# Interleaving the second DFT stage of ssm_k with the first DFT stage of kv, in one shared buffer

## The chip, the cores and the metric

The kernel runs on one core of a Trainium2 chip. The core has a matrix engine (TensorE, written PE below; its weight loads are written PEld), a vector engine (VectorE, DVE), an activation engine (ScalarE, ACT), a general engine (GpSimd, POOL) and a queue that starts the transfers (SyncE, SP). Every engine takes its instructions in the order in which the program wrote them, and waits where an operand isn't ready or a buffer isn't free. In this kernel TensorE reads its operands from the memory SBUF and writes its results to PSUM, in tiles of one or two banks (a bank holds 512 fp32 values in each of 128 partitions). DVE and ACT empty PSUM into SBUF; POOL works on data in SBUF alone.

The metric is the device time of one launch in microseconds (us). Before the change it was 207.4 us, the median of three runs from 207.04 to 207.55. A profile is one further execution. Its span was 204.4 us (206.56 us by the clock of the time measurement), so differences between points of the profile are read as differences of the time.

## The reference

Inputs are bf16, with 2048 tokens and 512 channels. The kernel computes a pre-normalised H3 block followed by a dense block:

```
ln(x)  = (x - mean) / sqrt(var + 1e-5)               over the channels
kv     = (sum_t shift(k, t) * shift_k[:, 3-t]) * v   4 causal taps
y      = irfft(rfft(pad(kv)) * rfft(pad(ssm_k)))[:2048]     length 4096, along the tokens
y      = bf16(y) + kv * ssm_D
h      = A_q + ln(A_q) * y
out    = h + relu(ln(h) @ w1) @ w2
```

The long convolution takes two forward transforms, one of the filter `ssm_k` and one of `kv`, a product of the spectra, and one inverse transform.

## The kernel before, in words

The kernel does each transform as two stages of matrix products. A row of 2048 values is seen as 64 rows of 32. Stage 1 (`stage1`) is a short transform over one index, with tables `f1`/`f2` kept as a bf16 high part and a bf16 low part, so that each result is a sum of two products. It gives 64 "planes" c: 32 frequencies k1, each with a real and an imaginary plane. Stage 2 (`stage2`) is a transform over the other index. For each k1 it multiplies the two planes of that k1, 128 partitions by 256 columns each, with 128x128 tables `cc`, `cs`, `cn` in the replicated fp32 format (fp32r), and gives the real part (s = 0) or the imaginary part (s = 1).

The order of the work is written by hand. The part around the change runs as follows.

1. Eight rounds of `taps` (the 4-tap convolution of k, times v) and `stage1(kfl, a1k, gb, ...)`, the first stage of ssm_k. Round gb writes columns 32*gb to 32*gb+31 of all 64 planes of `a1k`.
2. `to_rows` turns kv into the layout `xfl` with TensorE transposes.
3. The k4 loop: eight rounds of the second stage of ssm_k. Each round makes four k1, in two PSUM tiles `ps2k` of two banks. The tile of s = 0 is emptied by DVE, which adds `dcol` (the ssm_D term), and the tile of s = 1 by ACT; both go to `kf`, the spectrum of the filter.
4. Eight rounds `stage1(xfl, a1x, gb, ...)`, the first stage of kv. Each round fills two PSUM tiles `ps1` of two banks; ACT empties the first into `a1x` and DVE the second, through the helper `copy` (its lines appear in the profile as L258 for ACT and L260 for DVE). In round 4 the second tile is split between DVE and ACT.
5. The product stage: 16 rounds of `product(kp)` (second stage of kv into `u`, then the products with `kf` on DVE and POOL) and `finish` (sums into `psy`, emptied by ACT back into `kf`). Then the inverse transform and the dense block follow.

`a1k` and `a1x` are both tiles of 64 KB per partition from the pool `slotA`, which has one buffer. So the first write to `a1x` must wait until the last product of step 3 has read `a1k`: steps 3 and 4 can't overlap.

In steps 3 and 4 the four PSUM places `ring` = 1, 3, 2, 0, of two banks each, are given out in turn. A place can be written again when its eviction is done.

`stage1` has two forms. With `pairs=True` it works on 64 rows at a time: 8 groups x 2 tables x 2 halves = 32 products with 128 columns each. With `pairs=False` it works on 32 rows at a time: 8 x 2 x 4 = 64 products with 64 columns each. The four 32-row products, or the two 64-row ones, lie in different rows of TensorE's array. Step 4 uses pairs in rounds 1 to 7, and the 32-row form in round 0.

In the old plane order the real planes are c = k1 and the imaginary ones c = 32 + k1. `stage2` therefore reads planes k1 and 32 + k1, which lie 32 KB apart in each partition.

Of the kernel before, what the change touches and what calls it, by code (L numbers as in the profile page):

```python
# [12 lines left out]
F32R = mybir.dt.float32r  # L13
I32 = mybir.dt.int32
PSUM = bass.MemoryType.PSUM
P = 128
# [40 lines left out]
def kernel(  # L57
# [13 lines left out]
    nc = tc.nc  # L71
    _, S, D = A_q.shape
# [4 lines left out]
    DC = D // P  # L77
# [8 lines left out]
    slotA = pl.push("slotA")  # L86
# [52 lines left out]
    def _sin(out, turns, M, neg=False):  # L139

        nc.scalar.activation(out=out, in_=turns, func=ACT.Sin, scale=(-TURN if neg else TURN) / M,
                             bias=(pbias if neg else nbias)[:])
# [35 lines left out]
    def at_k1(tab, k1):  # L178
        a, t = [p for p in tab if p[0] <= k1][-1]
        return t[:, k1 - a, :]  # L180
# [25 lines left out]
    t1 = early.tile([P, 64], I32, name="f1_t")  # L206
    _turns(nc, t1[:, 0:32], r1[:], n1c[:], 128, True)
    _turns(nc, t1[:, 32:64], r1[:], n1c[:], 128, False)
    f1f = early.tile([P, 64], F32, name="f1_f")
    _sin(f1f[:, 0:32], t1[:, 0:32], 128)  # L210
    _sin(f1f[:, 32:64], t1[:, 32:64], 128, neg=True)
    t3 = early.tile([P, 2, 64], I32, name="dm_t")
    _turns(nc, t3[:, 0, :], r2[:, 32:96], n2s[:], 64, True)
    _turns(nc, t3[:, 1, :], r2[:, 32:96], n2s[:], 64, False)
# [9 lines left out]
    def cc_part():  # L224
        table(*cc_parts.pop(0))
# [21 lines left out]
    def negated(a, b):  # L247
        (ao, to), (ai, ti) = [[p for p in tab if p[0] <= a][-1] for tab in (cn, cs)]
        nc.gpsimd.tensor_single_scalar(out=to[:, a - ao:b - ao, :], in_=ti[:, a - ai:b - ai, :].bitcast(F32), scalar=-1.0,
                                       op=ALU.mult)  # L250
# [5 lines left out]
    def copy(eng, o, i):  # L256
        if eng == "A":
            nc.scalar.copy(out=o, in_=i)  # L258
        else:
            nc.vector.tensor_copy(out=o, in_=i)  # L260
# [9 lines left out]
    def bank2(name):  # L270
        return place([P, 2, 512], F32, name)
# [19 lines left out]
    def stage1(fl, a_out, gb, engs, pairs=False):  # L291

        pss = [bank2("ps1") for _ in range(2)]
        n, tabs = 2 if pairs else 4, (f2hi, f2lo) if pairs or fl is not kfl else (f1hi, f1lo)
        K = P // n
        for gi in range(8):
            for f in range(2):
                for t in range(n):
                    rows = slice(K * t, K * t + K)
                    cols = slice(0, P)  # L300
                    if pairs:
                        o = pss[t][:, gi // 4, 128 * (gi % 4):128 * (gi % 4) + 128]
                    else:
                        if fl is not kfl:
                            cols = slice(64 * (t % 2), 64 * (t % 2) + 64)
                        else:
                            cols = slice(0, 64)
                        o = pss[t // 2][:, t % 2, 64 * gi:64 * gi + 64]
                    nc.tensor.matmul(out=o, lhsT=fl[rows, 8 * gb + gi, :, :].rearrange("p d n -> p (d n)"),  # L309
                                     rhs=tabs[f][rows, cols], start=(f == 0), stop=(f == 1),  # L310
                                     tile_position=(K * t, 0), skip_group_check=True)
        for h in range(2):
            if pairs:
                src = pss[h][:].rearrange("p b (g r c) -> p c (b g) r", g=4, r=2)
            else:
                src = pss[h][:].rearrange("p r (g c) -> p c g r", c=64)
            dst = a_out[:, :, 32 * gb:32 * gb + 32].rearrange("p c (g r) -> p c g r", r=DC)[:, :, :, 2 * h:2 * h + 2]
            for g, eng in enumerate(engs[h]):
                n = 8 // len(engs[h])
                copy(eng, dst[:, :, g * n:g * n + n], src[:, :, g * n:g * n + n])  # L320

    def stage2(ps, a_in, kp, s):

        for kk in range(2):
            k1 = 2 * kp + kk
            w_re, w_im = ((cc, cs), (cn, cc))[s]
            nc.tensor.matmul(out=ps[:, kk, :], lhsT=at_k1(w_re, k1), rhs=a_in[:, k1, :], start=True, stop=False,  # L327
                             skip_group_check=True)
            nc.tensor.matmul(out=ps[:, kk, :], lhsT=at_k1(w_im, k1), rhs=a_in[:, 32 + k1, :], start=False, stop=True,  # L329
                             skip_group_check=True)  # L330


    kfl = early.tile([P, 64, 2, 64], BF16, name="kfl")
# [11 lines left out]
    dim = consts.tile([P, 2, 2, 64], F32R, name="dim")  # L345
    nc.gpsimd.memset(dre[:].bitcast(F32), 0.0)
    nc.gpsimd.memset(dim[:].bitcast(F32), 0.0)
    a1k = slotA.tile([P, 64, 256], F32R, tag="A", name="a1k")


    kvp2 = sk[:].rearrange("p c t -> p (c t)").rearrange("p (m c a e) -> p m c a e", m=32, c=DC, e=2)
    def taps(c, h):
        pss = [tap_bank(i, [P, 512], F32, "pkv") for i in range(2)]
        for i in range(2):
            for j in range(KS):
                nc.tensor.matmul(out=pss[i][:], lhsT=wdiag[:, 2 * h + i, j, :],  # L356
                                 rhs=kT[c][:, 2 * h + i, 16 - j:CH + 16 - j], start=(j == 0), stop=(j == KS - 1))
        for i in range(2):
            nc.vector.tensor_tensor(out=kvp2[:, :, 2 * h + i, 8 * c:8 * c + 8, :].rearrange("p m a e -> p a m e"),  # L359
                                    in0=pss[i][:].rearrange("p (a m e) -> p a m e", a=8, e=2),  # L360
                                    in1=vT[c][:, 2 * h + i, :].rearrange("p (a m e) -> p a m e", a=8, e=2),
                                    op=ALU.mult)

    for gb in range(8):
        taps(gb // 2, gb % 2)
        stage1(kfl, a1k, gb, ("AA", "AD")[gb % 2], pairs=(gb == 2))
        if gb < 6:
            cc_part()
        if gb == 1:
            negated(22, 32)  # L370
# [18 lines left out]
    xfl = xfp.tile([P, 64, 2, 64], BF16, name="xfl")  # L389
# [7 lines left out]
    for k4 in range(8):  # L397
        ks = slice(4 * k4, 4 * k4 + 4)
        for s in range(2):
            ps = bank2("ps2k")  # L400
            for h in range(2):
                stage2(ps[:, h, :].rearrange("p (k j) -> p k j", k=2), a1k, 2 * k4 + h, s)
            pj = ps[:].rearrange("p b (k j) -> p j (b k)", k=2)
            if s == 0:
                nc.vector.tensor_tensor(out=kf[:, 0, :, ks], in0=pj, in1=dcol, op=ALU.add)
            else:
                nc.scalar.copy(out=kf[:, 1, :, ks], in_=pj)

    a1x = slotA.tile([P, 64, 256], F32R, tag="A", name="a1x")
    for gb in range(8):  # L410
        stage1(xfl, a1x, gb, ("A", "DA" if gb == 4 else "D"), pairs=(gb > 0))
    pl.pop("psX")
    pl.pop("psF")
    pl.pop("xfp")
# [14 lines left out]
    def product(kp):  # L429
        ks = slice(2 * kp, 2 * kp + 2)  # L430
        kfr = kf[:].bitcast(F32)
        ts = []
        for s in range(2):
            u = psu.tile([P, 2, 256], F32, tag=f"u{s}", name=f"u{s}")
            stage2(u, a1x, kp, s)
            usb = prod.tile([P, 256 - NJ, 2], F32, tag=f"usb{s}", name=f"usb{s}", bufs=2)
            uj = u[:].rearrange("p k j -> p j k")
            nc.scalar.copy(out=usb[:], in_=uj[:, po, :])  # L438
            t = prod.tile([P, 2, 256, 2], F32R, tag=f"t{s}", name=f"t{s}")
            for eng, in0, j in ((nc.vector, uj[:, dv, :], dv), (nc.gpsimd, usb[:], po)):  # L440
                n = j.stop - j.start
                eng.tensor_tensor(out=t[:, :, j, :], in0=in0.unsqueeze(1).to_broadcast([P, 2, n, 2]),  # L442
                                  in1=kfr[:, :, j, ks], op=ALU.mult)
            ts.append(t)
        pending.append((kp, ts))
# [19 lines left out]
    for kp in range(16):  # L465
        product(kp)
        if kp >= LAG:
            finish(kp)
        if kp == 7:
            load_x(0)  # L470
            load_x(1)
        if kp == 10:
            w1 = wp.tile([P, DC, DFF], BF16, tag="c2s0", name="w1")
            nc.sync.dma_start(out=w1[:], in_=B_w1.rearrange("(c p) f -> p c f", p=P))
# [357 lines left out]
```

## Time and profile before

The profile's windows (busy time by engine in a stretch) give the stages from the second stage of ssm_k on:

| stretch of the profile, us | what runs | length | PE busy | DVE busy | ACT busy | POOL busy |
|---|---|---|---|---|---|---|
| 38.00 to 52.70 | step 3, second stage of ssm_k | 14.70 | 14.70 | 10.15 | 8.09 | 0.00 |
| 52.70 to 63.70 | step 4, first stage of kv | 11.00 | 8.77 | 9.50 | 10.04 | 0.80 |
| 63.70 to 94.50 | step 5, product stage | 30.80 | 30.72 | 27.38 | 25.25 | 28.24 |
| 94.50 to 114.00 | first inverse stage | 19.50 | 19.19 | 16.01 | 15.77 | 15.47 |
| 114.00 to 204.00 | second inverse stage, dense block | 90.00 | 85.92 | 51.13 | 41.09 | 13.83 |

A busy time is the union of an engine's instructions. Matmuls are pipelined: the start of one to the start of the next is what one costs in a stream, and its listed duration is longer than that. DVE and ACT instructions overlap their neighbours by a little too.

How to read a line of the timeline: start, length, engine, line of the kernel, operation, output<-inputs, shape, count, and in brackets how long the engine had been idle and what released it. A line of the chain: start, length, engine, output and line.

### The profile page before, as it was taken

Reading aid. Unit: us, or ns where it says so; the run is one execution under the profiler, and the core shown is the slowest. Engines: PE = TensorE matmul, PEld = TensorE weight load, DVE = VectorE, ACT = ScalarE, POOL = GpSimd, SP = SyncE. Lnnn points to the kernel's source line nnn. Section 1 sums busy time; section 2 is a strip of 40 time slices with the busy share of each in tenths; the row PEclk is TensorE's granted clock in tenths of the full one; section 3 lists DMA queues with packets and bytes.
Section 4 is the critical chain, followed back from the end, with each engine's and each line's share of the span. In section 5 each row is a group of like instructions: output and inputs, shape, how many; then the busy total and the mean of one; then the engine's idle time right before and its main releaser. Section 6 shows DMA issues by size and latency. Waiting matters only on the chain.

```text
span 204.4 us, 4868 instructions
## 1 busy us (share of the span) xinstructions
PE 194.5 (95%) x1985; PEld 138.0 (68%) x1985; DVE 146.0 (71%) x238; ACT 128.7 (63%) x198; POOL 86.6 (42%) x121
## 2 busy tenths in 40 slices
PE   7989999999997999999999999999999999999991
PEld 2565546999886898897998877545564556544451
DVE  7998777876787999888995698969387117661131
ACT  2768899655896798885979965844570593026300
POOL 7599993000004999996759475110211001002000
PEclk9999999999999999999999999999999999999999
DMA  5999970000000007808990658763483402140011
GB/s 175 343 225 192 192 138 5 3 0 3 5 3 2 0 3 189 264 27 208 203 277 4 109 103 155 138 131 103 92 108 89 116 0 51 32 108 17 0 51 51
DMA packets 48489, 20.01 MB, mean 98 GB/s; under 512 B 43380, under 2 KB 46932, under 8 KB 48468
## 3 DMA queue, kind: packets, MB, share of 16 engines
q1 hardware_dynamic: 47940, 19.71, 44.0%
q8 instruction: 15, 0.25, 0.5%
q10 hardware_dynamic: 528, 0.00, 0.1%
q14 instruction: 6, 0.05, 0.1%
HBM read 7.08 MB, written 2.10 MB: 45 GB/s over the span
## 4 chain that ended last, share of the span: by engine, by line
PE 83%; DVE 5%; ACT 5%; POOL 4%; issue 1%; POOLq 0%; ACTq 0%
PE ps1m L704 19%; PE ps2m L734 19%; PE psy L452 7%; PE psi L599 7%; PE pkv L356 6%; PE ps L309 4%; PE ps2k L327 4%; PE ps2k L329 4%; PE u L327 3%; PE u L329 3%; PE pz L677 3%; PE pst L280 2%; ACT c2s L193 1%; ACT a1x L258 1%; POOL wdiag L237 1%; DVE a1x L260 1%
## 5 line engine op out<-in xcount | busy, mean ns | idle before, releaser
L719 ACT ACTIVATE h1T<-ps1m 128x512 bf16<-128x512 f32 (+1 forms) x44 | 25.7, 597 | 35.8 <-PE ps1m L704 35.7
L704 PE MATMUL ps1m<-xT,w 128*128 128x512 bf16 (+2 forms) x192 | 43.7, 365 | 0.4 <-DVE xT L650 0.4
L734 PE MATMUL ps2m<-w,h1T 128*128 128x512 bf16 (+3 forms) x187 | 40.8, 368 | 0.0
L677 PE MATMUL pz<-bd,ax 128*128 128x128 f32 x96 | 35.7, 410 | 0.0
L442 POOL TENSOR_TENSOR t<-usb,kf 128x320 fp32r<-128x320 f32 x32 | 28.2, 944 | 2.1 <-ACT usb L438 1.7
L442 DVE TENSOR_TENSOR t<-u,kf 128x704 fp32r<-128x704 f32 x32 | 26.7, 886 | 3.1 <-ACT usb L438 3.0
L738 DVE SCALAR_TENSOR_TENSOR o<-ps2m,rstd,xh 128x512 bf16<-128x512 f32 (+1 forms) x17 | 12.1, 717 | 22.9 <-PE ps2m L734 11.5
L734 PEld LDWEIGHTS <-h1T 128*128 128x128 bf16 (+1 forms) x187 | 16.2, 98 | 16.0
L543 POOL TENSOR_SCALAR rstd<-mv 128x4 f32<-128x4 f32 x8 | 2.5, 316 | 56.5 <-DVE mv L541 56.5
L704 PEld LDWEIGHTS <-w 128*128 128x128 bf16 (+1 forms) x192 | 15.9, 100 | 12.1 <-DVE xT L650 0.5
L677 PEld LDWEIGHTS pz<-bd,ax 128*128 128x128 f32 x96 | 18.6, 193 | 7.6
L537 DVE BATCH_NORM_STATS2 st<-xh 128x6 f32<-128x512 bf16 x32 | 19.8, 676 | 0.0
L648 DVE TENSOR_TENSOR qT<-pz,qT 128x1024 bf16<-128x1024 f32 x8 | 9.8, 1220 | 13.6 <-PE pz L677 10.8
L258 ACT CAST kf<-psy 128x512 fp32r<-128x512 f32 x30 | 17.6, 647 | 1.9 <-PE psy L452 0.3
L527 ACT ACTIVATE bd<-ecw,nbias 32x512 fp32r<-32x512 int32 x24 | 17.3, 719 | 0.6
L452 PE MATMUL psy<-t,ipos 128*128 128x512 f32 x48 | 16.0, 393 | 0.0
L356 PE MATMUL pkv<-kT,wdiag 128*128 128x512 bf16 x64 | 15.2, 380 | 0.4 <-POOL f_lo L246 0.4
L258 ACT CAST ax<-psi 128x1024 fp32r<-128x1024 f32 x13 | 12.4, 1015 | 3.7 <-PE psi L599 3.7
L599 PE MATMUL psi<-dre,kf 128*128 128x256 f32 x60 | 14.6, 286 | 0.0
L599 PE MATMUL psi<-dim,kf 128*128 128x256 f32 x60 | 14.3, 280 | 0.0
L258 ACT CAST a1k<-ps 128x1024 fp32r<-128x1024 f32 x12 | 12.5, 1077 | 2.6 <-PE ps L309 2.6
L359 DVE TENSOR_TENSOR sk<-pkv,vT 128x512 bf16<-128x512 f32 x16 | 10.8, 689 | 4.4 <-PE pkv L356 4.2
(134 smaller groups left out, 415.4 us busy)
## 6 DMA issues: line engine op xcount, KB each, us to landing
sk<-in_A_ssm_k_dram SPq DMA_DIRECT2D x1, 2048.0 KB
xh<-in_A_q_dram SPq DMA_DIRECT2D x16, 128.0 KB
out_dram<-o SPq DMA_DIRECT2D x15, 128.0 KB
w<-in_B_w_dram SPq DMA_DIRECT2D x1, 1376.0 KB
w<-in_B_w_dram SPq DMA_DIRECT2D x1, 1280.0 KB
xh<-xT SPq DMA_TRANSPOSE x8
out_dram<-o SPq DMA_DIRECT2D x2, 64.0 KB
w<-in_B_w_dram SPq DMA_DIRECT2D x1, 96.0 KB
```

What stands on the lines that cost most here:

```text
L258: nc.scalar.copy(out=o, in_=i)
L327: nc.tensor.matmul(out=ps[:, kk, :], lhsT=at_k1(w_re, k1), rhs=a_in[:, k1, :], start=True, stop=False, skip_group_check=True)
L356: nc.tensor.matmul(out=pss[i][:], lhsT=wdiag[:, 2 * h + i, j, :], rhs=kT[c][:, 2 * h + i, 16 - j:CH + 16 - j], start=(j == 0), stop=(j == ...
L442: eng.tensor_tensor(out=t[:, :, j, :], in0=in0.unsqueeze(1).to_broadcast([P, 2, n, 2]), in1=kfr[:, :, j, ks], op=ALU.mult)
L452: nc.tensor.matmul(out=psy[:], lhsT=m_[:], rhs=t_.rearrange("p j k -> p (j k)"), start=first, stop=not first)
L527: nc.scalar.activation(out=bd[h][rows, :, :, rg, :], in_=ecw[q % 2][rows, :, 256 * h:256 * h + 256].rearrange("p b (j n) -> p b j n", n=32 ...
L537: nc.vector.bn_stats(out=st[:, i, :], in_=src[:, i, :])
L599: nc.tensor.matmul(out=banks[i // 2][:, i % 2, :], lhsT=kf[:, c, 4 * m:4 * m + 4, :].rearrange("p r k -> p (r k)"), rhs=d[:].rearrange("p ...
L677: nc.tensor.matmul(out=pz[:, il, :, a, :], lhsT=ax[:, 64 * rho + n2, :, :].rearrange("p d g -> p (d g)"), rhs=bd[h][:, rho, 4 * il + a, :, ...
L704: nc.tensor.matmul(out=ps1[fc][:fsz, 128 * ii.start:128 * ii.stop].rearrange("p (i t) -> p i t", t=P), lhsT=w1[:, c, fc * P:fc * P + fsz], ...
L719: nc.scalar.activation(out=h1T[:fsz, fc, :], in_=ps1[fc][:fsz, :], func=ACT.Relu)
L734: nc.tensor.matmul(out=ps2[:, 0:w], lhsT=h1T[:ksz, fc, i * P:(i + 1) * P], rhs=w2[:ksz, fc, ds], start=(fc == 0), stop=(fc == NFC - 1))
```

## The change

The change puts the first stage of kv into the k4 loop. After the two tiles of the second stage of ssm_k for four k1, the loop makes one eighth of the first stage of kv (`gb = k4`). To make that possible in one buffer,

- the planes are reordered so that the real and the imaginary plane of one k1 are neighbours, c = 2*k1 and 2*k1 + 1 (the columns of the table `f1` are written in that order);
- `a1k` and `a1x` become two views of one tile `a1`. As `a1k` it is planes of 256 columns one after the other, so round k4 of the second stage reads planes 8*k4 to 8*k4+7, which are elements 2048*k4 to 2048*k4+2047. As `a1x` it is eight blocks of 2048 elements, one for each gb, with 64 planes of 32 columns in each. So block gb = k4 is free as soon as round k4 has read it;
- the product stage reads a plane of `a1x` as 8 runs of 32 elements, 2048 elements apart, where it was one run of 256;
- all eight groups of kv use the 32-row form, and the split of the second tile between DVE and ACT is made in rounds 2 and 5, not in round 4 alone.

```diff
     f1f = early.tile([P, 64], F32, name="f1_f")
-    _sin(f1f[:, 0:32], t1[:, 0:32], 128)
-    _sin(f1f[:, 32:64], t1[:, 32:64], 128, neg=True)
+    f1p = f1f[:].rearrange("p (k s) -> p s k", s=2)
+    _sin(f1p[:, 0], t1[:, 0:32], 128)
+    _sin(f1p[:, 1], t1[:, 32:64], 128, neg=True)
...
-            dst = a_out[:, :, 32 * gb:32 * gb + 32].rearrange("p c (g r) -> p c g r", r=DC)[:, :, :, 2 * h:2 * h + 2]
+            dst = a_out(gb).rearrange("p c (g r) -> p c g r", r=DC)[:, :, :, 2 * h:2 * h + 2]
...
-            nc.tensor.matmul(out=ps[:, kk, :], lhsT=at_k1(w_re, k1), rhs=a_in[:, k1, :], start=True, stop=False,
+            nc.tensor.matmul(out=ps[:, kk, :], lhsT=at_k1(w_re, k1), rhs=a_in(2 * k1), start=True, stop=False,
                              skip_group_check=True)
-            nc.tensor.matmul(out=ps[:, kk, :], lhsT=at_k1(w_im, k1), rhs=a_in[:, 32 + k1, :], start=False, stop=True,
+            nc.tensor.matmul(out=ps[:, kk, :], lhsT=at_k1(w_im, k1), rhs=a_in(2 * k1 + 1), start=False, stop=True,
...
-    a1k = slotA.tile([P, 64, 256], F32R, tag="A", name="a1k")
+    a1 = slotA.tile([P, 64 * 256], F32R, tag="A", name="a1")
+
+    def a1k_of(gb):
+        return a1[:].rearrange("p (c j) -> p c j", j=256)[:, :, 32 * gb:32 * gb + 32]
+
+    def a1k(c):
+        return a1[:, 256 * c:256 * c + 256]
+
+    def a1x_of(gb):
+        return a1[:, 2048 * gb:2048 * gb + 2048].rearrange("p (c j) -> p c j", j=32)
+
+    def a1x(c):
+        return a1[:].rearrange("p (b c j) -> p b c j", b=8, j=32)[:, :, c, :]
...
-        stage1(kfl, a1k, gb, ("AA", "AD")[gb % 2], pairs=(gb == 2))
+        stage1(kfl, a1k_of, gb, ("AA", "AD")[gb % 2], pairs=(gb == 2))
...
             else:
                 nc.scalar.copy(out=kf[:, 1, :, ks], in_=pj)
-
-    a1x = slotA.tile([P, 64, 256], F32R, tag="A", name="a1x")
-    for gb in range(8):
-        stage1(xfl, a1x, gb, ("A", "DA" if gb == 4 else "D"), pairs=(gb > 0))
+        stage1(xfl, a1x_of, k4, ("A", "DA" if k4 in (2, 5) else "D"))
...
-            stage2(u, a1x, kp, s)
+            stage2(u[:].rearrange("p k (b j) -> p k b j", b=8), a1x, kp, s)
```

## The prediction

> **What bounds the kernel now.** I read the busy time by stretch first, then the chain that ended last where the two stages meet, then the groups by shape in that stretch, then single lines of the timeline for the costs.
>
> By stretch (length, then busy time of PE, PEld, DVE, ACT, POOL):
>
> ```profile
> 38.00:52.70 14.70, 14.70 (x131) 14.62 (x129) 10.15 (x10) 8.09 (x10) 0.00 (x0) 1.00 0.00 1
> 52.70:63.70 11.00, 8.77 (x290) 7.33 (x289) 9.50 (x9) 10.04 (x10) 0.80 (x2) 1.00 0.02 4
> 63.70:94.50 30.80, 30.72 (x193) 27.15 (x194) 27.38 (x33) 25.25 (x62) 28.24 (x32) 1.00 0.33 96
> ```
>
> In the second stage of ssm_k (first line) PE never stops, and DVE and ACT are idle for 4.6 and 6.6 us. In the first stage of kv (second line) it is the other way round: DVE and ACT are nearly full, and PE waits. The product stage (third line) is full on PE again. The chain across the meeting point shows the turn:
>
> ```profile
> 52.75 0.13 PE ps2k L329
> 52.88 0.02 issue
> 52.90 1.02 ACT kf L407
> 53.92 0.04 issue
> 53.96 1.06 PE ps L309 x31
> 55.03 1.09 ACT a1x L258
> 56.12 0.04 issue
> 56.16 2.36 PE ps L309 x64
> 58.52 1.56 ACT a1x L258 x2
> 60.08 0.04 issue
> 60.13 1.06 PE ps L309 x31
> 61.19 0.02 issue
> 61.21 2.37 DVE a1x L260 x2
> 63.58 0.14 issue
> 63.72 0.36 PE u L327
> ```
>
> After 52.88 the end is set by turns of eviction and refill of PSUM. An eviction's end frees a place for PE 0.04 us later, and `u` starts 0.14 us after the last eviction. So 25.65 us (38.07 to 63.72) go to two stages whose busy times complement each other: summed over both, PE 23.5, DVE 19.7, ACT 18.1.
>
> **What the Trainium skill says.** (1) "TensorEngine Tiling (Array Packing)", Key Properties: going from one tiling of the array to another, not only to another tile, drains TensorE. The change has 15 such turns in the loop. The trace agrees, and shows a small price:
>
> ```profile
> 52.59 0.28 PE L329 MATMUL ps2k<-a1k,c2c 128*128 128x256 f32 x1
> 52.80 0.21 PE L309 MATMUL ps<-f_hi,xfl 32*128 32x64 bf16 x4
> 53.41 0.23 PE L309 MATMUL ps<-f_hi,xfl 64*128 64x128 bf16 x1
> ```
>
> A 256-column product takes 0.113 us, so it is done issuing at 52.70; the 32-row group begins at 52.80, a turn of 0.10. The whole 32-row group, with the turn out of it, takes 0.61 (52.80 to 53.41). The pairs groups take 1.06 between turns.
> (2) "SBUF — State Buffer", Specifications: lines of 16 bytes, at least two hits per line for full rate. The runs of 32 fp32 are 128 bytes, eight whole lines, so by this page they cost nothing. The trace has a harder case that agrees: the transposes of ssm_k read single fp32 values 128 bytes apart and start every 0.120 us (ten in 1.35 with a last one of 0.27), those of kv read contiguous ones every 0.113 (eight in 1.06).
> (3) "PSUM — Partial Sum Buffer", PSUM bank collisions: two engines may not read one bank of a partition together. So where a tile is split "DA", the ACT half waits for the DVE half. The trace agrees: the DVE half of round 4 ran 58.56 to 59.24, and the ACT half ended at 60.08, which is what PE waited for.
>
> **The change part by part.** The new table order, the two views and the strides of the first-stage writes change no instruction count and no element count, and in the innermost loops of the writes pairs of adjacent values stay 16 bytes apart: zero. Seven groups of kv go from 32 products of pairs to 64 of 32 rows, so PE gets 448 more instruction entries; at 0.61 for a group of 128 of them, as ssm_k's rounds and kv's round 0 run, that is already counted.
>
> PE, one round of the loop: 16 second-stage products x 0.113 = 1.81; a turn 0.10; the group 0.61; and the first fp32 weight load, which can't be hidden after a turn. The first products of the stage started at 38.07 and 38.29, so that costs 0.22 - 0.11 = 0.11. Sum 2.63 per round.
>
> DVE, one round: `kf` 1.22 and the second kv tile 1.22, which start 1.13 apart if both are waiting (two in 2.35). ACT: `kf` 1.01 and the first kv tile 1.11. Both sums (2.35 and 2.1) lie under PE's 2.63, so they can hide, but the four PSUM places are now used once per round each, and the circuits must be checked. An eviction starts 0.20 after PE has moved on to the next group:
>
> ```profile
> 48.17 0.28 PE L327 MATMUL ps2k<-a1k,c2n 128*128 128x256 f32 x1
> 48.37 1.22 DVE L405 TENSOR_TENSOR kf<-ps2k,dtab 128x1024 fp32r<-128x1024 f32 x1 [0.59 <-PE ps2k L329]
> 53.64 1.23 DVE L260 CAST a1x<-ps 128x1024 fp32r<-128x1024 f32 x1 [0.42 <-PE ps L309]
> ```
>
> and 0.23 after the kv group (53.41 to 53.64).
> - Place of `kf` s = 0: filled at 1.02, evicted from 1.22, but not before DVE is through with the kv tile of the round before: 0.23 + 1.13 = 1.36. End 2.58, free at 2.63. PE wants it at 2.63. It just fits.
> - Place of s = 1: ACT from 2.12 to 3.13; wanted at 2.63 + 1.02 = 3.65. Fits.
> - First kv tile: ACT is busy until 3.1, then to 4.2; wanted at 2.63 + 2.0 = 4.6. Fits.
> - Second kv tile: DVE from 2.86 to 4.08. Fits. In rounds 2 and 5 its ACT half queues behind the first tile, 4.15 to 4.73, so PE waits some 0.1 at the next kv group. Behind that wait only kv's own group stands; `kf`'s next products come after it. Twice, with their effect on the rest: 0.2.
>
> So PE sets the pace. From 38.07: sixteen tiles of eight products 16 x 0.905, eight kv groups with their turn 8 x 0.71, eight weight loads 8 x 0.11; 14.5 + 5.7 + 0.9 = 21.0, and 0.2 gives the end of the last kv group at 59.3. The tail: ACT is still on `kf` until 0.5 after that, then 1.1 for the first kv tile: 60.9, plus 0.14 to `u` = 61.1 instead of 63.7. That is 2.6 us less. Unlike in the old order the tail's evictions are two, not a backlog.
>
> The first kv group can't begin earlier than its input: `xfl` is complete at 39.0, the group starts at 40.1. No wait.
>
> Product stage: the 128 products now read 8 runs. It is full on PE (30.72 of 30.80), so any price is paid in full. From below zero; from above, seven jumps at the 0.007/128 us per jump of the strided transposes are under 0.001 us each product, 0.05 in all. The dense block's moving operand in four runs of 128 shows no price either (first dense stage 9.50/44 = 0.216 a product). I take zero. A jump of 8 KB within a stream of fp32r products isn't in the trace, so I keep up to 0.01 us a product (1.3 us) for the range. Everything after that stage hangs on its end and moves with it, transfers included, since these are released by the product stage's own reads. 207.4 - 2.6 = **204.8**.
>
> **The rivals.**
> - *Turns cost more in this mix* (no fp32 round around a 32-row group exists in the trace twice in a row): at 0.25 a turn in and 0.2 for the weight load the round is 2.87, 1.9 us more over eight, against which the tail shortens a little (ACT is done with `kf` sooner): about 206.4. For it: only one turn of this kind is in the trace. Against: the eight turns between taps and groups in bf16 cost under 0.1 each (period 2.45 for 8 x 0.216 + 0.61).
> - *The PSUM circuit becomes the bound*: the DVE place has no slack. If evictions start 0.35 after the group and not 0.20, the s = 0 circuit gives about 2.73 a round, 0.8 more: 205.6. For it: the first eviction of the stage started 0.35 after. Against: the other seven were at 0.20.
> - *The broken-up reading costs* (ends slower): at 0.03 us a product, 128 x 0.03 = 3.8, time 207.4 + 3.8 - 2.6 = 208.6. For it: PE is full there, and the same fp32r product takes 0.116 there against 0.113 in ssm_k's second stage, so its speed isn't the same in all surroundings. Against: the strided transposes.
> - *Turns hide better than seen*: weight load pulled ahead, 8 x 0.1 less: 204.2.
>
> **How the numbers follow.** Forecast (204.2 to 205.4) 0.6; turns dearer 0.12; PSUM circuit 0.1; broken-up reading 0.1, most of it slower than before; better than 204.2 0.08. The range from 203.7 to 206.5 holds the forecast, the cheap end and both milder rivals, and leaves out the strong form of the reading's price. Faster by over 0.3% means under 206.8: 0.87; same 0.05; slower 0.08.
>
> **What would show it.** In the profile after, `ps2k` and `ps<-xfl` alternate from about 38 us, with rounds of 2.6 to 2.7; the first `u` starts near 61.1; PE's waits in the loop are few and short, the longest before the kv groups of rounds 3 and 6; DVE and ACT are both over 80% busy in the loop. The product stage keeps its length (`u` to the end of `psy` 30.8) and `u` products stay 0.116 apart, and all later stages keep theirs. The forecast is wrong if a round takes 2.9 or more (turns: PE idle with nothing to wait for; circuit: idle released by DVE `kf`), or if the product stage lengthens by over 0.5 us.

## The result, and the profile after

The kernel after takes 204.56 us (204.17 to 205.06, four runs) against 207.48 us for the kernel before (207.04 to 207.75, four runs on the same chip): ratio 0.9863, 95% interval 0.9833 to 0.9892, so 2.9 us less. The forecast was 204.8. The profiled span went from 204.4 to 202.2 us. Some executions fall into a slower state: a median below is that of all runs of a kernel, while each ratio, with its interval, is taken from the fast runs alone.

The windows of the kernel after (stretch, length, then busy time of PE, PEld, DVE, ACT, POOL with instruction counts, PE's clock, DMA share, GB/s) for the loop, the product stage and the rest:

```profile
38.61:61.41 22.80, 21.32 (x643) 19.92 (x641) 18.86 (x18) 17.98 (x20) 0.80 (x2) 1.00 0.02 4
61.41:92.30 30.89, 30.85 (x193) 27.36 (x194) 27.37 (x33) 25.06 (x62) 28.25 (x32) 1.00 0.32 94
92.30:202.20 109.90, 105.16 (x748) 68.43 (x745) 67.26 (x127) 56.93 (x84) 29.35 (x32) 0.99 0.50 96
```

The first of these stretches in the kernel before:

```profile
38.07:63.72 25.65, 23.40 (x419) 21.95 (x417) 19.57 (x18) 18.06 (x19) 0.80 (x2) 1.00 0.01 3
```

From the first `ps2k` to the first `u` there were 25.65 us before; now there are 22.80, which is 2.85 less. That is the whole gain. The other two stretches keep their lengths (30.80 and 109.9 before). In the one profile the loop started 0.54 later than in the profile before, which is why the span shrank by 2.2 and not by 2.9. That start varies between 38.1 and 39.7 over the profiles of this study; in the latest of them, and in this one too, the chain ahead of the loop leads back to the input transfers.

The meeting of one round with the next, in PE's timeline:

```profile
43.13 0.28 PE L330 MATMUL ps2k<-a,c2c 128*128 128x256 f32 x1
43.33 0.21 PE L310 MATMUL ps<-f_hi,xfl 32*128 32x64 bf16 x4
43.37 0.20 PE L310 MATMUL ps<-f_lo,xfl 32*128 32x64 bf16 x4
...
43.95 0.38 PE L328 MATMUL ps2k<-a,c2c 128*128 128x256 f32 x1
44.17 0.28 PE L330 MATMUL ps2k<-a,c2s 128*128 128x256 f32 x1
44.28 0.28 PE L328 MATMUL ps2k<-a,c2c 128*128 128x256 f32 x1
```

The last product of the second stage is through at 43.24 (one takes 0.11), so the turn into the 32-row group costs 0.09. The group with the turn out of it takes 0.62 (43.33 to 43.95), and the first weight load that can't be hidden 0.22 - 0.11 = 0.11. No line has a bracket, so PE waited for nothing. Rounds start at 38.61, 41.30, 43.95, 46.57, 49.23, 51.92, 54.56 and 57.22, so they take 2.62 to 2.69; the second-stage products in them are 0.113 to 0.118 apart.

PE waits once from the loop's start to the product stage, at its end. The view of its waits, and the chain there (start, length, engine, output, line):

```profile
PE u L328 <- ACT a L259: 1.5, 1, 1.5
```

```profile
59.20 0.13 PE ps2k L330
59.33 0.02 issue
59.35 1.01 ACT kf L420
60.36 0.99 ACT a L259
61.35 0.05 issue
61.41 0.38 PE u L328
```

Of the turns of eviction and refill that made up the old chain from 52.88 to 63.72, one is left.

### The profile page after: what moved, and what is told of

Same layout as the page of the kernel before. It is cut to its first block, busy times and chain, and to the rows that moved or that the text cites. A ratio compares the mean times of both kernels' runs of the same rounds, so it can differ in the third digit from the quotient of the medians.

```text
span 202.2 us, 5318 instructions
## 1 busy us (share of the span) xinstructions
PE 192.2 (95%) x2209; PEld 136.3 (67%) x2209; DVE 144.8 (72%) x238; ACT 128.6 (64%) x199; POOL 85.5 (42%) x121
## 4 chain that ended last, share of the span: by engine, by line
PE 78%; SPq 11%; DMA 3%; DVE 3%; ACT 2%; issue 1%; ACTq 0%
PE ps1m L714 19%; PE ps2m L744 19%; PE psy L462 7%; PE psi L609 7%; PE ps2k L328 4%; SPq L118 4%; SPq L115 4%; PE ps2k L330 4%; PE u L328 4%; PE u L330 3%; SPq L117 3%; DMA kT<-in_A_k_dram 3%; PE pz L687 3%; PE ps L310 2%; PE pst L281 2%; PE pkv L369 2%
## 5 line engine op out<-in xcount | busy, mean ns | idle before, releaser
L748 DVE SCALAR_TENSOR_TENSOR o<-ps2m,rstd,xh 128x512 bf16<-128x512 f32 (+1 forms) x17 | 12.1, 717 | 22.2 <-PE ps2m L744 11.5
L259 ACT CAST a<-ps 128x1024 fp32r<-128x1024 f32 (+1 forms) x22 | 22.4, 1054 | 3.6 <-PE ps L310 3.6
L261 DVE CAST a<-ps 128x1024 fp32r<-128x1024 f32 (+1 forms) x12 | 13.6, 1137 | 2.6 <-PE ps L310 2.5
```

## The experiments

### The two halves apart

The change does two things to kv's first stage: it interleaves it, and it puts it into 32-row products. Each was run alone. Interleaving alone:

```diff
-        stage1(xfl, a1x_of, k4, ("A", "DA" if k4 in (2, 5) else "D"))
+        stage1(xfl, a1x_of, k4, ("A", "DA" if k4 in (2, 5) else "D"), pairs=(k4 > 0))
```

> The new order, but kv's groups 1 to 7 as 32 products of 64 rows, as before the change. Theory of the prediction (TensorE sets the round): a round costs 16 x 0.113 + two turns and a weight load 0.21 + 1.06 = 3.08 us, so 7 x 0.45 = 3.2 us come back, and the first u starts near 63.9 us after a start of the loop at 38.07: 207.5 us, level with the kernel before. Rival A (the interleaving alone gives the gain, the smaller products are incidental): at most 205.5 us.

Measured: 207.02 against 207.34, ratio 0.9995 (0.9976 to 1.0015). Interleaving alone gains nothing. Its rounds start 3.01 to 3.02 apart (PE's timeline):

```profile
41.04 0.38 PE L328 MATMUL ps2k<-a,c2c 128*128 128x256 f32 x1
...
44.05 0.38 PE L328 MATMUL ps2k<-a,c2c 128*128 128x256 f32 x1
...
47.07 0.38 PE L328 MATMUL ps2k<-a,c2c 128*128 128x256 f32 x1
```

With pairs PE has 23.82 us of work in a stretch of 25.26 (38.38 to 63.64), so the loop is nearly as long as the two stages were one after the other (25.65). The 64-row groups are too dear on an engine that is now the bound.

32-row products alone, in the kernel before:

```diff
-        stage1(xfl, a1x, gb, ("A", "DA" if gb == 4 else "D"), pairs=(gb > 0))
+        stage1(xfl, a1x, gb, ("A", "DA" if gb == 4 else "D"))
```

> The kernel before, with all of kv's groups as 64 products of 32 rows and nothing else changed. Theory: in the old order that stage waits for evictions, ACT's eight tiles at 1.06 plus a half of 0.55 from 53.9 on, so u starts at about 63.1 instead of 63.7: 206.8 us, 0.6 less. Rival B (the smaller products alone give the gain): 7 x 0.45 less, 204.3 us.

Measured: 212.26 against 207.34, ratio 1.0258 (1.0195 to 1.0321). The expectation was wrong by 5.5 us, and by its sign. To see whether the old layout had a part in it, the same order was run on the layout of after:

```diff
-        stage1(xfl, a1x_of, k4, ("A", "DA" if k4 in (2, 5) else "D"))
+    for gb in range(8):
+        stage1(xfl, a1x_of, gb, ("A", "DA" if gb == 4 else "D"))
```

> The kernel after, with kv's eight groups taken out of the loop again into a loop of their own: new plane order, new layout, broken-up reading and 32-row products, but the old order of stages. Theory (layout and reading cost nothing): like the kernel before with 32-row products, 206.8 us, and u products 0.116 us apart. Rival C (the broken-up reading costs something that the gain hides): slower than that run by 128 times the price, 1.3 us at 0.01.

Measured: 213.49, ratio 1.0267 (1.0181 to 1.0353): the same loss on both layouts, and the same miss, since this expectation was made with the same cost of a group. So the two halves need each other: neither 207.4, interleaved only 207.0, 32 rows only 212.3, both 204.6.

What takes the time is seen in PE's timeline of the kernel with 32-row products alone. These lines stand in the middle of a group, where no operand and no buffer is outstanding:

```profile
57.94 0.21 PE L309 MATMUL ps<-f_lo,xfl 32*128 32x64 bf16 x4 [0.93 <-issue]
...
61.66 0.21 PE L309 MATMUL ps<-f_lo,xfl 32*128 32x64 bf16 x4 [1.53 <-issue]
...
65.39 0.24 PE L309 MATMUL ps<-f_lo,xfl 32*128 32x64 bf16 x4 [1.30 <-issue]
```

PE resumes 3.72 and 3.73 us apart. PE's windows between (busy time and number of products, clock, DMA share, GB/s):

```profile
57.93:61.65 3.72, 1.57 (x128) 1.00 0.02 4
61.65:65.38 3.73, 1.88 (x128) 0.59 0.02 4
```

It ran 128 products in each. A product is two instruction entries, a weight load and a multiplication, so that is 256 entries. The Trainium skill, "Runtime: NRT & Kernel Launch", section "Instruction fetch mechanics", says that an engine's instructions are fetched in blocks of 16 KiB, which are 256 instructions, while it executes the block before, and that this is mostly hidden. The block of 256 agrees with the trace; that it is hidden doesn't hold here. The theory formed on this was: TensorE is fed at most one block per 3.7 us, 69 entries per us. A group of 128 entries is executed in 0.61 us, and groups that follow each other at the pace of the evictions (about 1.2 us) want some 107 per us. The old pairs wanted half of that. In the loop of after a round has 160 entries (16 slow and 64 fast products) in 2.65 us, 60 per us.

The blocks themselves are in the trace. Windows of PE in the kernel with 32-row products alone show them in the last column (GB/s), as little else is transferred here:

```profile
55.50:56.70 1.20, 0.86 (x84) 1.00 0.06 14
56.70:59.05 2.35, 1.27 (x127) 1.00 0.00 0
59.05:60.35 1.30, 0.61 (x36) 1.00 0.06 13
```

13 to 14 GB/s over these lengths are some 17 KB, one block. In the records of the instruction queue (q8), transfers of 16384 bytes start at 55.55, 59.07 and 62.80. PE resumes 2.39, 2.59 and 2.59 us after each of them, and the next one starts 1.13 and 1.14 after PE has resumed. So 3.7 us is one turn of asking for a block and taking it up, and while PE waits no second block is on its way. In the kernel after, five such transfers start in the loop, 3.5 to 5.0 us apart, and PE doesn't wait for them.

A second loss follows from the first. Windows of the same kernel around the end of the stage (the clock is the third number from the end):

```profile
57.00:61.70 4.70, 1.61 (x133) 1.31 (x136) 2.47 (x3) 2.95 (x4) 0.00 (x0) 1.00 0.02 3
61.70:63.50 1.80, 1.25 (x102) 1.08 (x106) 1.35 (x2) 1.39 (x2) 0.00 (x0) 0.67 0.04 9
63.50:67.40 3.90, 1.15 (x64) 0.86 (x62) 2.23 (x2) 1.87 (x2) 0.80 (x2) 0.50 0.01 2
67.40:71.00 3.60, 3.60 (x17) 3.60 (x18) 2.00 (x3) 0.88 (x3) 1.95 (x3) 0.50 0.02 5
```

PE was busy for 1.61 of 4.70 us, and then its clock fell to half. The Trainium skill, "TensorE: Matmul & The Clock Gate", section "What's actually happening", gives half the clock after an idle window of about 3.4 us, and the whole again after as long a busy one. The trace agrees on the half (0.50), and shows that it can fall where PE wasn't wholly idle, and that the whole came back 5.0 us after the full work began. The clock was still down when the product stage began: `u` products were 0.21 apart and not 0.117 until about 72 us. In sum, the stage from the last `ps2k` to `u` took 14.13 us (53.27 to 67.40) where it took 10.97 before, 3.2 more, and the slow products some 2 more: that is about the 4.9 by which the median is longer. The profiled run was the longest of its four, 7.6 over the profiled run before; besides these two losses its loop started 0.5 later, and PE waited 2.0 in the inverse stage for DVE, which it doesn't before.

### The supply of instructions, tested

If the supply is the limit, then the loop of after must starve too once its groups are made twice over, though nothing else in it changes:

```diff
-            for f in range(2):
+            for f in (0, 1) if fl is kfl else (0, 1, 0, 1):
```

> The kernel after with every kv group's products made twice over (the second set starts anew and leaves the same sums): 128 more instruction entries and 0.61 us more of TensorE per round, the same evictions. Theory, TensorE is fed about 256 entries per 3.7 us: a round of 16 slow products and 256 fast ones is 288 entries and takes 4.2 us instead of 3.26, with waits on 'issue' inside the groups; over 8 rounds, less what is in store at the start, 8 to 11 us over the kernel after: 212 to 215. Rival, the waits of the kernels with the groups back to back came from something else (the evictions, the space's buffers): a round costs 2.65 + 0.61 = 3.26 us, with no wait on 'issue': 209.4.

Measured: 217.04 against 207.67, ratio 1.0440 (1.0394 to 1.0486). That is 12.5 over the kernel after (12.0 by the two ratios), where PE's added work alone is 4.9. The waits are back, inside the groups (PE's timeline), and PE again runs a block between one and the next (PE's windows, busy time and count):

```profile
48.73 0.21 PE L310 MATMUL ps<-f_lo,xfl 32*128 32x64 bf16 x4 [0.39 <-issue]
...
52.46 0.21 PE L310 MATMUL ps<-f_lo,xfl 32*128 32x64 bf16 x4 [0.54 <-issue]
...
56.29 0.19 PE L310 MATMUL ps<-f_hi,xfl 32*128 32x64 bf16 x1 [0.64 <-issue]
...
60.02 0.18 PE L310 MATMUL ps<-f_hi,xfl 32*128 32x64 bf16 x1 [0.52 <-issue]
```

```profile
48.72:52.45 3.73, 3.19 (x128) 1.00 0.02 4
52.45:56.28 3.83, 3.19 (x127) 1.00 0.02 4
56.28:60.01 3.73, 3.21 (x128) 1.00 0.02 4
```

The mix of slow and fast products differs from the run before, and so do the buffers and the evictions; the block of 128 products in 3.73 us is the same (one record of the second window is missing). The stalls move through the round, since 288 entries a round is no multiple of 256. The list of queues on the page of the profile counts the blocks, packets first:

```profile
q8 instruction: 17, 0.28, 0.6%
```

```profile
q8 instruction: 21, 0.34, 0.7%
```

The first is after, the second this kernel: four blocks more are 1024 entries, eight rounds of 128. The transfers of the instruction queue start at 46.30, 49.87, 53.59, 57.45 and 61.65, and PE resumes 2.4 to 2.7 us after each. The loop takes 34.27 us (39.07 to 73.34), 11.5 more than after, where the theory allowed 8 to 11. In it stands one wait on "issue" of 2.3 us, longer than the 0.4 to 0.6 of the others: the block ahead of it held fast products almost alone and was done in 1.7 us, and its successor was asked for 1.63 us after PE had resumed, not 1.13 to 1.16. After that wait the clock fell here too, to 0.50 from 65 to 68 us. What each of the two adds isn't separated.

The other side: in the old order, 32 rows in every other group only.

```diff
-        stage1(xfl, a1x, gb, ("A", "DA" if gb == 4 else "D"), pairs=(gb > 0))
+        stage1(xfl, a1x, gb, ("A", "DA" if gb == 4 else "D"), pairs=(gb % 2 == 1))
```

> The kernel before (old order) with 32-row products in kv's groups 0, 2, 4 and 6 and 64-row products in 1, 3, 5 and 7. Theory of supply: 768 entries at 69 per us are 11.1 us, of which the store at the start gives some 150 entries (2 us), so that the evictions of about 10 us set the stage's end: hardly a wait on 'issue', TensorE's clock stays whole, and the time is 206.8 to 207.6. Rival, a 32-row group outside the loop costs some 0.7 us more than a 64-row group whatever stands around it (the loss of 4.9 us over seven groups): three more of them than before, 209.5.

Measured: 208.85 against 207.67, ratio 1.0046 (1.0025 to 1.0066), between the two expectations. The time alone decides nothing; the stage itself does (windows from the last `ps2k` to the first `u`, this kernel and then the kernel before):

```profile
54.40:65.46 11.06, 7.75 (x385) 6.64 (x385) 9.43 (x9) 9.81 (x10) 0.80 (x2) 1.00 0.02 4
```

```profile
52.75:63.72 10.97, 8.72 (x290) 7.36 (x289) 9.45 (x9) 10.04 (x10) 0.80 (x2) 1.00 0.02 4
```

Its length is that of before. PE has no wait on "issue" in it and keeps its clock, with 768 entries in 11.06 us, 69 per us, just at the limit. So a 32-row group outside the loop isn't slow by itself. The stage began 1.65 later in this profile, because the loads at the start came later; the runs of this kernel spread from 206.9 to 209.4 and further. Whether the edit has a part in that isn't settled.

### The price of a turn

The forecast allowed 0.10 for a turn in and 0.11 for the exposed weight load, from one place in the trace before. Here one 32-row product is put ahead of every `ps2k` tile of the kernel with two loops, into a place that is then overwritten:

```diff
             ps = bank2("ps2k")
+            nc.tensor.matmul(out=ps[:, 0, 0:64], lhsT=ident[0:32, :], rhs=f2hi[0:32, 0:64], start=True, stop=True,
+                             tile_position=(0, 0), skip_group_check=True)
```

> The two-loop kernel, with one 32-row product of 64 columns set ahead of each of the sixteen tiles of ssm_k's second stage; it writes a corner of the tile that the next products overwrite, so the result stays the reference's. Its use is to add sixteen turns into the 32-row form and out of it. Theory: each costs 0.10 + 0.11 and the product 0.03, 16 x 0.24 = 3.8 us more than the two-loop kernel, 210.6 us. Rival (turns are free, and the 0.71 of a kv group is issue time of its 128 entries): 16 x 0.03, 207.3 us.

Measured: 219.3, ratio 1.0553 (1.0462 to 1.0644), some 5.9 over the kernel with two loops by the two ratios. PE's timeline:

```profile
45.30 0.28 PE L330 MATMUL ps2k<-a,c2s 128*128 128x256 f32 x1
45.51 0.20 PE L414 MATMUL ps2k<-f_hi,ident 32*128 32x64 bf16 x1
45.64 0.39 PE L328 MATMUL ps2k<-a,c2n 128*128 128x256 f32 x1
45.86 0.28 PE L330 MATMUL ps2k<-a,c2c 128*128 128x256 f32 x1
```

0.21 - 0.11 = 0.10 for the turn in, 0.13 for the product with the turn out, 0.22 - 0.11 = 0.11 for the load: 0.34 together, where 0.24 were expected: the way out had been left out, and it is a third of the whole. Sixteen make 5.4, and the second stage of ssm_k did grow from 14.72 to 20.07 us between the two profiles. In the loop of after the way out is part of the group's 0.61, so nothing is missing from its sum; but with fewer products between turns the price would stand out.

### The broken-up reading

The forecast took the reading in eight runs of 32 values for free, on the ground that transposes of single values 128 bytes apart ran at nearly the full pace. Here the layout of an eighth is changed, so that a plane is 256 single values, 256 bytes apart:

```diff
-        return a1[:, 2048 * gb:2048 * gb + 2048].rearrange("p (c j) -> p c j", j=32)
+        return a1[:, 2048 * gb:2048 * gb + 2048].rearrange("p (j c) -> p c j", j=32)
...
-        return a1[:].rearrange("p (b c j) -> p b c j", b=8, j=32)[:, :, c, :]
+        return a1[:].rearrange("p (b j c) -> p c b j", b=8, j=32)[:, c]
```

> The kernel after, with the values of a block of kv's first stage stored the other way round (column major), so that the product stage reads a plane as 256 single fp32 values, 256 bytes apart, where it read 8 runs of 32. It takes the suspected price of broken-up reading to its extreme. Theory (the strided transposes showed 0.007 us on 128 values): u products 0.116 to 0.13 us apart, time 204.5 to 206.3. Rival, the 16-byte lines of the skill's SBUF page, which would be hit once each: reading at half the rate or less, u products 0.2 us apart or more, 128 x 0.1 = 13 us or more slower.

Measured: 232.44 against 207.44, ratio 1.1203 (1.1169 to 1.1236). The first block is PE's timeline of after, the second of this kernel:

```profile
70.04 0.28 PE L328 MATMUL u<-a,c2n 128*128 128x256 f32 x1
70.16 0.28 PE L330 MATMUL u<-a,c2c 128*128 128x256 f32 x1
70.28 0.28 PE L328 MATMUL u<-a,c2n 128*128 128x256 f32 x1
```

```profile
79.90 0.48 PE L328 MATMUL u<-a,c2c 128*128 128x256 f32 x1
80.20 0.48 PE L330 MATMUL u<-a,c2s 128*128 128x256 f32 x1
80.49 0.48 PE L328 MATMUL u<-a,c2n 128*128 128x256 f32 x1
```

0.29 a product against 0.12. The pace is the same from 70 to 76 us, where TensorE's granted clock was 0.50 (products start at 70.09, 70.38, 70.67), while the contiguous `u` products above slowed from 0.117 to 0.21 at that clock: what limits these products isn't TensorE's clock. For 256 values that is 1.13 ns each; the strided transposes ran at 0.120 for 128 values, 0.94 ns each. They were already slow, so they were no evidence for a free reading. Why their contiguous partners, at 0.113, aren't faster, no run here shows. The evictions suffered as well, as their pairs of values were no longer neighbours: 2.14 us on DVE and 2.12 on ACT in the mean of this loop (1.96 to 2.37), against 1.23 and 1.09. The loop took 28.31 us, 5.5 more than after, and `u` started at 67.46.

Two more layouts, runs of 2 values and runs of 4, with the pairs kept together for the evictions (the lines for the evictions' writes and the shape of `u` change with them):

```diff
-        return a1[:, 2048 * gb:2048 * gb + 2048].rearrange("p (c j) -> p c j", j=32)
+        return a1[:, 2048 * gb:2048 * gb + 2048].rearrange("p (g h c e) -> p c g h e", g=8, h=2, e=2)
...
-        return a1[:].rearrange("p (b c j) -> p b c j", b=8, j=32)[:, :, c, :]
+        return a1[:].rearrange("p (x c e) -> p x c e", x=128, e=2)[:, :, c, :]
...
```

> The kernel after with each eighth of the space laid out in runs of 2 values instead of 32: the evictions write the same pairs of neighbours as before, and a product of the product stage reads its plane as 128 runs of 2 values (8 bytes), 512 bytes apart. Theory, the Trainium skill's page 'SBUF - State Buffer' on 16-byte lines taken at its word, two hits to a line being enough: products stay 0.118 us apart, evictions 1.1 to 1.2 us, the time 204.6. Rival, the price follows the share of a line that is used: between 0.12 and the 0.29 us of single values, about 0.2 us, and with 128 such products some 10 us more: 214. If the evictions stay at 1.1 to 1.2 us, the 2.0 us of the run with single values came from writing singles.

Measured: 226.38 against 207.67, ratio 1.0897 (1.0847 to 1.0948). Products were 0.29 apart, as with single values; the evictions were back at 1.23 and 1.10 us and `u` at 61.5, so the 2.1 us above came from writing singles. The Trainium skill, "SBUF — State Buffer", Specifications, asks for at least two hits per line of 16 bytes for full bandwidth. Two were not enough here.

For runs of 4, a whole line, the two views become

```diff
+        return a1[:, 2048 * gb:2048 * gb + 2048].rearrange("p (g c r) -> p c g r", g=8, r=4)
...
+        return a1[:].rearrange("p (x c r) -> p x c r", x=64, r=4)[:, :, c, :]
...
```

> The kernel after with each eighth of the space laid out in runs of 4 values (16 bytes): a product of the product stage reads its plane as 64 whole runs of 4 values, 1 KB apart; the evictions write pairs of neighbours as before. Runs of 2 values cost as much as single ones, 0.29 us a product. Theory, what counts is that a whole line of 16 bytes is used: products stay 0.118 us apart and the time is 204.6. Rival, every jump costs what it cost with runs of 2, (0.29 - 0.117) / 128 = 1.35 ns: 64 of them make 0.20 us a product, and 128 products 11 us more, 215.5.

Measured: 207.34 against 207.09, ratio 1.0013 (0.9992 to 1.0035): between the two expectations. PE's timeline:

```profile
70.22 0.32 PE L333 MATMUL u<-a,c2s 128*128 128x256 f32 x1
70.37 0.31 PE L331 MATMUL u<-a,c2n 128*128 128x256 f32 x1
70.52 0.31 PE L333 MATMUL u<-a,c2c 128*128 128x256 f32 x1
```

0.147 a product: nearly all of the price is gone with whole lines, but not all of it. 0.147 - 0.117 is 0.03 for 64 runs, some 0.5 ns a run. At that rate the eight runs of the change cost 0.004 a product, 0.5 us over 128 of them; from the first `u` to the end of the stage after has 0.09 more than before (30.89 against 30.80). Distances other than 256, 512 and 1024 bytes, and the 8 KB of the change itself, weren't tried, so how far these prices hang on the distance stays open.

### The evictions and the places

Three edits of the loop's other resources. The split of kv's second tile taken out of rounds 2 and 5:

```diff
+        stage1(xfl, a1x_of, k4, ("A", "D"))
```

> The kernel after, with no tile split between DVE and ACT in rounds 2 and 5. Theory: DVE's circuit of 2.58 fits the round of 2.63 without it, so 204.3 to 204.6, no difference to be measured. Rival (the split keeps DVE's queue from building up): DVE falls behind, TensorE waits for the place of kf s = 0, 205 us or more.

Measured: 204.74 (204.5 to 204.93), ratio 0.9875 (0.9850 to 0.9900): no different from after. DVE then has 19.75 us of work in a loop of 22.85, which still fits. And the split in every round:

```diff
+        stage1(xfl, a1x_of, k4, ("A", "DA"))
```

> The kernel after, with kv's second tile split between DVE and ACT in every round. Theory: ACT then has 1.01 + 1.11 + 0.6 less overlaps = 2.6 a round, its half of the tile comes free at the time at which TensorE wants it, waits of some 0.1 before most kv groups and a longer tail: 205.2 us. Rival (evictions have slack enough): as the kernel after, 204.5.

Measured: 206.27, ratio 0.9942 (0.9922 to 0.9961), so 1.7 slower than after, and more than expected. ACT is then busy for 21.14 of 23.46 us, and the tail is longer, since after the last `kf` it has both halves to do (1.59 us from 61.52). The loop explains 0.7; the rest lies ahead of the loop, which in this profile began at 39.7, and no run tells what part of it belongs to the edit.

One of the four PSUM places taken away ahead of the loop:

```diff
         to_rows(lambda m: kv32[:, m, :], q, xfl, "DADDADAD"[q])
+    ring[:] = [1, 3, 2]
     pl.pop("early")
     pl.pop("vp")
```

> The kernel after, with three PSUM places in the loop in place of four. Theory (four places fit with no slack to spare): the second kv tile then waits for DVE's eviction of kf s = 0 in the same round, about 0.6 us a round, 4.8 in all: 209.4 us, and TensorE's idle time is released by DVE and ACT. Rival (PSUM places have slack): 204.5 to 205.5.

Measured: 211.86, ratio 1.0228 (1.0185 to 1.0271). The loop takes 28.26 us (38.60 to 66.86) instead of 22.80, and PE's waits in it are those of the PSUM circuit, which the forecast named as a rival:

```profile
PE ps2k L328 <- ACT kf L421: 1.0, 5, 0.3
PE ps L310 <- DVE kf L419: 0.6, 2, 0.4
```

The loop grew by 5.5, of which 1.6 are such waits; PE's busy time grew as well, from 21.32 to 24.31 with the same products, and what of this is waiting booked as work these views don't separate. Beyond the loop PE's clock was 0.90 from 100 to 117 us in this profile, which is part of the rest. With four places none of these waits occurs.

## Why the prediction was right, step by step

- *A round of 2.63*: right, 2.62 to 2.69. Turn 0.09, group 0.62, load 0.11, sixteen products of 0.113 to 0.118. The 0.11 of the load had been read at the stage's first product, ahead of which there is no turn; after a turn it is the same (43.95 to 44.17). The run with added turns shows the same terms.
- *DVE and ACT hide, the circuit of s = 0 just fits*: right. PE waited for no eviction in the loop. With three places it does.
- *Waits of 0.2 in rounds 3 and 6*: these didn't come. The forecast put the ACT half of round 2 at 4.73 after the start of its round; it ended at 48.58, which is 4.63 after 43.95, just in time for the group of round 3. The groups of rounds 3 and 6 took 0.64 instead of 0.61, and no more than that can be a wait. Taking the split out changed nothing that could be measured. The forecast also said that the ACT half waits for the DVE half, and that the trace agrees. The trace doesn't show that: ACT worked without a pause from 57.38 to 62.29 in the profile before, so its half stood behind its own tiles.
- *A tail of 0.5 + 1.1 + 0.14*: measured 0.43 + 0.99 + 0.06. This is why the loop shrank by 2.85 and not by 2.6. The missing waits don't explain it, since the slower products used them up: eight rounds took 21.25 us (from 38.61 to the last group, which began at 59.25, and its 0.61), where the forecast had 21.0 and 0.2 of waits.
- *The broken-up reading at zero*: right in size, 0.09 us measured, but for a wrong reason. The transposes held up as the harder case that ran free were not free. Runs of 32 are cheap because they are long: 8 of them, of whole lines.
- *448 more entries, "already counted"*: this is where the forecast was lucky. The group's 0.61 had been read in ssm_k's rounds, where eight slow products stand between groups (144 entries in 2.45 us, 59 per us), and in kv's single round 0. It didn't ask whether the duration would hold at a higher rate of entries. In the loop, at 60 per us, it does. With the same groups back to back it doesn't, and the expectation for that kernel, made with the same 0.61, missed by 5.5 us. Interleaving does more than fill idle engines: its slow products give the fetch the time to follow (256 entries in 4.2 us at 60 per us, against the 3.7 of a turn).

## What to carry to other kernels

Before small products are packed back to back, count their instruction entries per microsecond: here TensorE got 256 per 3.73 us, and a group that took 0.61 us alone couldn't be repeated every 1.2 us. Waits on "issue" in the middle of a group, a constant time between them, and a fixed number of instructions in that time are its mark; slow products placed between are the cure. A duration carries over only with its surroundings, and a slow case that seems free beside another slow case proves nothing.

## What the hardware did that was not expected

- TensorE ran dry of instructions: 128 products (256 entries) per 3.72 to 3.83 us, in two kernels with different mixes of products. The next block of 16 KiB was asked for 1.1 us after PE had taken up the last, and came into use 2.4 to 2.7 us later.
- Its clock fell to 0.50 after 4.7 us in which it was busy for 1.61, and `u` products took 0.21 until about 5 us into the full work that followed.
- Reading a moving fp32r operand of 256 values: 0.116 in one run, 0.118 to 0.120 in 8 runs, 0.147 in 64 runs of 4, 0.29 in 128 runs of 2 as in 256 single values, and still 0.29 for single values at half the clock.
- Evictions of 1024 values that wrote single values instead of pairs took 2.1 us in the mean instead of 1.1 to 1.2.
